# Mask rows, unread products and expert 0's input in place in attention; one pair of banks for transposed rows and rows in front of a block

## The chip, the core and the metric

The kernel runs on one core of one Trainium2 chip. Its engines work side by side, each through its own instructions in order: PE (TensorE, products and transposes; PEld are its weight loads), DVE (VectorE), ACT (ScalarE), POOL (GpSimd), and SP (SyncE), which here only issues DMA transfers. An engine that waits for something holds back all that stands behind in its program. The metric is the time of one execution in microseconds of the device, as a median of several runs. PE's clock has two levels, 1.2 and 2.4 GHz; the profile gives the granted one as a share of the higher.

## The reference, cut to what matters

Three layers in a row: attention in which a query sees only the keys of its own cluster, a mixture of 8 experts with one expert for each token, and a gated unit with a product before and after it.

```
q_assign = argmax(q_n @ c_n), k_assign = argmax(k_n @ c_n)      # 16 clusters, for each head
mask     = q_assign[:, :, :, None] == k_assign[:, :, None, :]
scores   = where(mask, q @ k.T / sqrt(64), -1e9)                # 2 x 8 heads, 768 x 768
x        = softmax(scores) @ v                                  # -> (1536, 512)
e        = argmax(x @ w_gate);  h = relu(x @ w1[e]);  y = gate * (h @ w2[e])    # 8 experts, 512 -> 1024 -> 512
out      = (silu(y @ wg) * (y @ wv)) @ wo                       # 512 -> 1536 -> 512
```

## The kernel before, in words

All arithmetic is in float32, made of float32r products of a high and a low part (names ending in H/L or h/l): a product is done as high times high plus the two mixed ones.

Attention takes the 16 heads as 8 pairs (n) of two heads (r). A head has six blocks of 128 queries; `run` (class Attention) goes through 96 of these blocks, called groups g: six of one head, then six of the other. In each group it emits steps in the order CFG['order']: S (`soft`: exponential of block g+1 on ACT), E (`evac`: result of three blocks, on ACT and DVE), Q (`qk`: score product of block g+2 on PE and its maximum on DVE), T0 and T1 (`pt`: transposes of the exponentials on PE, copied by ACT and DVE), B0 (first step of a list `bg[g]`), O (`onat`), V0 (`pv`, every third group: product with v), B1 (the other steps of `bg[g]`). A score product adds the mask by further rows of its operands: one-hot cluster rows in tiles Bq and Bk (qB, kB). For the second head of a pair these rows must stand on other partitions than the transposes leave them, so they are copied to a tile oT and moved by DMA (`move`, L150).

The list `bg` holds the preparation of pair n+1 (`prep_steps`: k0, q0, q1, k1 transposes of the loaded tiles ldq and ldk, L169; a, t, f the cluster choice; m0, m1 the mask rows), at offsets from CFG['offs'], for pair 1 from CFG['offs1'] (its q is prepared before the first group), and the load of the pair after it. k0 of pair 2 stands in group 9. Pair 0 is prepared ahead of the loop: `mask0` makes its mask rows, `unit` fetches the gate's weights by six small transfers, `moves` places the high and low parts of pair 1's q. `warm` emits products that nobody reads.

SP issues all moves and loads in program order. All of them are on one queue.

In groups 81 to 92 the weights of expert 0 arrive in eight chunks (raw tiles, a ring of NRAW = 4) and are split into high and low halves by `piece(i, k, eng)`: chunk i, half k, the high part copied by ACT (eng 1) or POOL (eng 0), the low part always made by POOL. The list `pieces` hangs at step E, `spare` at given groups. `head` fetches the first 128 tokens of expert 0 (which the router has scattered to moe_rows) into a raw tile, `turn_head` transposes them, `take_head` splits them into the tile XA. `tail` then computes these tokens (`head1`, `head2`) while the last tokens are scattered.

Experts (`run` of class Experts): for each expert four products l1, two l2, and between them `xt`, which transposes the rows of the next expert into two PSUM tiles of two banks each (a ring of four) and splits them into X. `split(e, i)` splits chunk i of expert e and then issues the load of the chunk four places on into the freed raw tile; `rows(e, t)` fetches rows of the expert after next. The gated unit (class Glu) follows.

Of the kernel before, what the change touches and what calls it, by code (L numbers as in the profile page):

```python
# [23 lines left out]
class Attention:  # L24
# [253 lines left out]
    def mask0(self):  # L278
# [23 lines left out]
        keys(*ps[1])  # L302
        queries(*ps[0])
        for sl, flat in ps:
            nc.vector.tensor_copy(st["oT"][q, sl], flat[q])
            nc.scalar.activation(out=st["oT"][k, sl], in_=flat[k], func=AF.Identity, scale=self.sc[k, 0:1],
                                 bias=self.sc[k, 1:2])
        for si, nm in enumerate("qk"):
            r0 = 2 * si * C
            self.move(st["B" + nm][64 - C:64, 1], st["oT"][r0 + C:r0 + 2 * C])  # L310

    def mask(self, n, half):
# [190 lines left out]
    def run(self, cent, gate, early, fill, after, spare, pieces, go):  # L503
# [6 lines left out]
        for n in range(1, self.NP):  # L510
            s0 = 2 * J * (n - 1)
            st = self.prep_steps(n)
            for nm, o in CFG["offs" if n > 1 else "offs1"]:
                if n == 1 and nm in ("q0", "q1"):
                    continue
                bg.setdefault(s0 + o, []).append(st[nm])
            if n + 1 < self.NP:
                bg.setdefault(s0 + CFG["load"], []).append(lambda n=n: self.load(n + 1, "qk"))
            if n > 1:
                bg.setdefault(s0 + 5, []).append(lambda n=n: self.load(n, "v"))  # L520
# [16 lines left out]
        self.warm(self.ps_m, "mm", 18)  # L537
        self.mask0()
        self.unit(gate)
        early()  # L540
        self.unit2()
        low()
        self.moves(1, 0, "q")
        self.moves(1, 1, "q")
        for e in range(self.E + 1):
# [4 lines left out]
        self.soft(0)  # L550
        self.qk(1)

        chains, moves, ready = [], [], {}
# [87 lines left out]

CFG = {'px': 'a', 'mt2': ['S', 'E', 'Q', 'T0'], 'mt': ['B1'], 'pt': 'V0', 'pe': 1, 'ms': [5, 2, 2], 'mr': 5, 'order': ['S', 'E', 'Q', 'T0', 'T1', 'B0', 'O', 'V0', 'B1'], 'offs': [['k0', -3], ['q0', -2], ['q1', -1], ['k1', 0], ['a', 1], ['t', 3], ['f', 6], ['m0', 7], ['m1', 8]], 'xe': 'da', 'me': 'a', 'ee': 'a', 'ec': 1, 'oc': [5, 5, 2], 'offs1': [['q0', 4], ['k0', 0], ['k1', 1], ['a', 2], ['t', 3], ['f', 5], ['m0', 6], ['m1', 7], ['q1', 0]], 'load': 0}

# [252 lines left out]
class Experts:  # L896
# [63 lines left out]

    def split(self, e, i):
        if e >= self.E:
# [5 lines left out]
        j = (nc.vector if e and i < 4 else nc.gpsimd).tensor_tensor(out=l, in0=t, in1=h.bitcast(F32), op=ALU.subtract)  # L968
        if e:
            for n in {8: [10], 9: [11], 10: [12], 11: [13], 12: [14, 15, 16]}.get(8 * e + i, [8 * e + i + NRAW]):  # L970
# [5 lines left out]
    def piece(self, i, k, eng):  # L976
# [7 lines left out]
        if k == 1:  # L984
            del self.loads[0, i]
            (lambda: self.load(4), self.head, self.slots, lambda: self.load(5), lambda: self.load(6), lambda: None,
             lambda: None)[i]()

    def head(self):

        rt = self.rt
        t = self.raw.tile([128, 4, 256], F32, tag="raw", name="raw").rearrange("p a b -> p (a b)")[:, 0:self.DM]
        i = self.nc.sync.dma_start(out=t, in_=rt.rows[rt.first:])
# [3 lines left out]
        self.xa = t  # L997

    def slots(self):
        self.XA = self.raw.tile([128, 2, self.KD, 128], F32R, tag="raw", name="XA")  # L1000

# [69 lines left out]
    def tail(self, at, go):  # L1071
# [17 lines left out]
        go(12)  # L1089
        a = self.fold(1)  # L1090
        rt.after(self.split(0, 7), [end])
        for _ in a:
# [66 lines left out]
    def xt(self, e, cnt):  # L1159
        nc = self.nc  # L1160
        banks = [self.bank("xp") for _ in range(self.KD // 2)]
        nt = 2 if self.late(e) else 3

        def turn(t, k):
            x = self.x3 if t == 2 else self.xr[e][:, t]
            return nc.tensor.transpose(banks[k // 2][:, k % 2, t * 128:(t + 1) * 128], x[:, k * 128:(k + 1) * 128], self.ident)

        def body(w):
            w = min(w, nt * 128)
            for a, b in ((0, 2), (2, 4)):  # L1170
                h, l = [self.X[:, i, a:b, 0:w] for i in range(2)]
                ps = banks[a // 2][:, a % 2:a % 2 + b - a, 0:w]
                nc.scalar.copy(out=h, in_=ps)
# [116 lines left out]
    def run(self, hook):  # L1290
# [5 lines left out]
        for e in range(E):  # L1296
# [5 lines left out]
            for mp in range(4):  # L1302
# [7 lines left out]
                if mp and mp < 3 and not e:  # L1310
                    self.split(1, mp - 1)
            if e:
                self.split(e, 6)
            if e == 5:
                rt.tokens(self.bank("xp")[:, 0, 0:2 * rt.B * rt.J])
            self.arms(e, cnt, lambda w: self.hidden(3, ps, w))
            if e + 1 < E:
                self.xt(e + 1, then)
                self.rows(e + 2, 0)
            if e:  # L1320
                self.split(e, 7)
# [181 lines left out]
def tile_clustered_attention_moe_swiglu(ctx, tc, q, k, v, cent, gate, w1, w2, wg, wv, wo, out, cap):  # L1503
# [7 lines left out]
    with tc.manual_schedule():  # L1511
        ident = const.tile([128, 128], F32, name="ident")
        with ExitStack() as c2:
# [3 lines left out]
            with ExitStack() as c1:  # L1517
# [12 lines left out]
                def first():  # L1530
# [8 lines left out]
                L = lambda i: lambda: ex.load(i)  # L1539
                pieces = [P(1, 1, 1), P(2, 0, 1), P(3, 1, 1), P(4, 0, 1), P(5, 1, 1), P(6, 0, 1)]  # L1540
                spare = {g0: [first], g0 + 1: [L(1), P(0, 0, 0)], g0 + 2: [L(2), P(0, 1, 0)], g0 + 3: [L(3), P(1, 0, 0)],
                         g0 + 5: [P(2, 1, 0)], g0 + 6: [P(3, 0, 0)], g0 + 8: [P(4, 1, 0)],
                          g0 + 9: [at.most, P(5, 0, 0), L(7)], g0 + 10: [lambda: None, lambda: ex.turn_head(at)],
                         g0 + 11: [ex.take_head, P(6, 1, 0)]}
                go = lambda n, it=ex.head1(at): [next(it) for _ in range(n)]
# [44 lines left out]
```

## Time and profile before

| | us |
|---|---|
| median of 3 runs | 753.95 (753.9 to 755.81) |
| profiled execution | 752.9 |
| its span | 751.2 |
| PE busy | 731.3 (97%) |
| DVE, ACT, POOL busy | 509.4, 394.5, 280.3 |
| granted clock of the span | 0.997 |

Attention takes the first 283 us of the span, the experts run until 446, the gated unit to the end. The span is the time between the first and the last instruction of the profile; the execution's own time is 1.7 us more. "Busy" counts an engine's instructions alone, so an engine can be 97% busy and slow all the same where its clock is halved. A row of the timeline gives the start, the duration, the engine, the line, the result and the operands, how many instructions were merged, and in brackets how long the engine stood idle before it and what ended that.

### The profile page before, as it was taken

Reading aid. Unit: us, or ns where it says so; the run is one execution under the profiler, and the core shown is the slowest. Engines: PE = TensorE matmul, PEld = TensorE weight load, DVE = VectorE, ACT = ScalarE, POOL = GpSimd, SP = SyncE. Lnnn points to the kernel's source line nnn. Section 1 sums busy time; section 2 is a strip of 40 time slices with the busy share of each in tenths; the row PEclk is TensorE's granted clock in tenths of the full one; section 3 lists DMA queues with packets and bytes.
Section 4 is the critical chain, followed back from the end, with each engine's and each line's share of the span. In section 5 each row is a group of like instructions: output and inputs, shape, how many; then the busy total and the mean of one; then the engine's idle time right before and its main releaser. Section 6 shows DMA issues by size and latency. Waiting matters only on the chain.

```text
span 751.2 us, 12723 instructions
## 1 busy us (share of the span) xinstructions
PE 731.3 (97%) x4310; PEld 608.7 (81%) x4310; DVE 509.4 (68%) x863; ACT 394.5 (53%) x763; POOL 280.3 (37%) x267
## 2 busy tenths in 40 slices
PE   7999999999999999999999999999999999999996
PEld 6777777767776789999999998788888888888885
DVE  4667777688787756666676567866766677676333
ACT  6777686877768754666667534542332222232110
POOL 6120211212125854555694334343333322333245
PEclk9999999999999999999999999999999999999999
DMA  9857869547256337688877733232122111210012
GB/s 203 176 137 205 203 181 250 129 108 173 48 157 205 101 125 241 220 253 267 264 248 239 217 116 106 89 89 80 57 67 74 57 57 56 85 29 0 1 57 112
DMA packets 103790, 102.92 MB, mean 137 GB/s; under 512 B 30896, under 2 KB 90800, under 8 KB 103696
## 3 DMA queue, kind: packets, MB, share of 16 engines
q1 hardware_dynamic: 101632, 95.37, 45.9%
q0 software_dynamic: 1920, 6.29, 2.2%
q8 instruction: 56, 0.92, 0.5%
q14 instruction: 38, 0.31, 0.1%
q10 hardware_dynamic: 144, 0.03, 0.0%
HBM read 68.48 MB, written 12.85 MB: 108 GB/s over the span
## 4 chain that ended last, share of the span: by engine, by line
PE 50%; DVE 4%; issue 3%; ACT 3%; POOL 1%; DMA 1%; DVEq 0%; ACTq 0%; POOLq 0%; SPq 0%
PE o L1456 12%; PE g L1438 12%; PE v L1438 12%; PE yp L1223 4%; PE hp L1223 3%; PE yp L1215 2%; PE hp L1215 2%; PE yp L1224 2%; PE hp L1224 1%; ACT W1h L967 1%; DVE gtmp L1415 1%; POOL out L1467 1%; DMA raw<-in_moe_w 1%; DVE gtmp L1414 0%; DVE hp L1237 0%
## 5 line engine op out<-in xcount | busy, mean ns | idle before, releaser
L368 DVE TENSOR_REDUCE nm<-s 128x1 f32<-128x768 f32 x96 | 91.1, 950 | 12.3 <-PE s L365 10.9
L968 POOL TENSOR_TENSOR W2l<-raw,W2h 128x1024 fp32r<-128x1024 f32 x29 | 69.1, 2396 | 66.8 <-ACT W2h L967 66.6
L378 ACT ACTIVATE P<-s,nm 128x768 f32<-128x768 f32 x96 | 86.6, 902 | 12.1 <-DVE nm L368 11.7
L397 PE MATMUL t<-ident,P 128*128 128x128 f32 x576 | 81.2, 275 | 0.9 <-ACT PT L400 0.7
L1445 POOL TENSOR_TENSOR ghl<-u,ghh 128x512 fp32r<-128x512 f32 x36 | 50.1, 1392 | 76.1 <-ACT ghh L1444 76.1
L397 PEld LDWEIGHTS t<-ident,P 128*128 128x128 f32 x576 | 68.9, 141 | 7.6 <-DVE PT L402 2.0
L416 PE MATMUL acc<-PT,ldv 128*64 128x384 f32 x384 | 69.2, 495 | 0.0
L1464 DVE TENSOR_TENSOR acc<-o,acc 128x512 f32<-128x512 f32 x60 | 41.5, 692 | 33.1 <-PE o L1456 32.9
L1223 PE MATMUL yp<-H,W2h 128*128 128x256 f32 (+3 forms) x224 | 61.7, 354 | 2.0 <-DVE H L1244 1.3
L365 PE MATMUL s<-Ak,Aq 128*128 128x384 f32 x192 | 58.8, 387 | 4.6 <-ACT P L378 3.8
L1223 PE MATMUL hp<-X,W1h 128*128 128x256 f32 (+3 forms) x224 | 61.0, 352 | 1.2 <-PE yp L1224 0.8
L1442 DVE TENSOR_TENSOR u<-sg,g 128x512 f32<-128x512 f32 x36 | 24.8, 688 | 54.8 <-ACT sg L1441 52.0
L400 ACT COPY PT<-t 128x384 f32<-128x384 f32 x96 | 45.7, 476 | 27.3 <-PE t L397 27.1
L1444 ACT CAST ghh<-u 128x512 fp32r<-128x512 f32 x36 | 22.4, 621 | 68.3 <-DVE u L1443 68.3
L1224 PE MATMUL yp<-H,W2l 128*128 128x128 f32 (+3 forms) x224 | 54.2, 242 | 0.0
L1224 PE MATMUL hp<-X,W1l 128*128 128x128 f32 (+3 forms) x224 | 54.0, 241 | 0.1
L402 DVE COPY PT<-t 128x384 f32<-128x384 f32 x96 | 52.4, 546 | 0.9 <-PE t L397 0.9
L968 DVE TENSOR_TENSOR W1l<-raw,W1h 128x1024 fp32r<-128x1024 f32 x28 | 43.3, 1565 | 13.8 <-ACT W1h L967 13.5
L365 PEld LDWEIGHTS s<-Ak,Aq 128*128 128x128 f32 x192 | 29.2, 190 | 28.6 <-ACT P L378 17.7
L365 PE MATMUL s<-kB,qB 80*128 80x384 f32 (+1 forms) x192 | 50.4, 343 | 0.3 <-issue 0.2
L416 PEld LDWEIGHTS acc<-PT,ldv 128*64 128x64 f32 x384 | 25.1, 136 | 28.0 <-issue 27.1
L176 POOL TENSOR_TENSOR Lk<-Xk,Hk 128x384 fp32r<-128x384 f32 x14 | 14.0, 1003 | 89.6 <-ACT Xk L175 89.6
(303 smaller groups left out, 1932.2 us busy)
## 6 DMA issues: line engine op xcount, KB each, us to landing
raw<-in_moe_w SPq DMA_DIRECT2D x64, 512.0 KB, 5.0
Ak<-Hk SPq DMA_DIRECT2D x32, 192.0 KB, 4.4
moe_rows<-zero SPq DMA_DIRECT2D x8, 768.0 KB, 5.3
raw<-in_moe_w_gate SPq DMA_DIRECT2D x12, 512.0 KB, 3.6
raw<-in_moe_w_val SPq DMA_DIRECT2D x12, 512.0 KB, 3.8
raw<-in_moe_w_out SPq DMA_DIRECT2D x12, 512.0 KB, 3.6
xr<-moe_rows SPq DMA_DIRECT2D x17, 256.0 KB, 4.1
ldq<-in_q SPq DMA_DIRECT2D x16, 192.0 KB, 4.1
```

The lines of the kernel that those rows point to most:

```text
L365: nc.tensor.matmul(ps[:, c, 0:HS], lhsT=ql[:, qs], rhs=kr[:, c * HS:(c + 1) * HS], start=a == 0, stop=a == 1)
L368: nc.vector.tensor_reduce(out=nm, in_=ps[:, :, 0:HS], axis=AX.XY, op=ALU.max, negate=True)
L378: nc.scalar.activation(out=P, in_=ps[:, :, 0:HS], func=AF.Exp, bias=nm, accum_out=self.pairs[n]["sum"][:, i, r:r + 1])
L397: nc.tensor.transpose(ps[:, jj, :], P[:, a, jj * 128:(jj + 1) * 128], self.ident)
L402: nc.vector.tensor_copy(PT[:, js, cs], ps)
L416: nc.tensor.matmul(acc[c * D:(c + 1) * D], lhsT=v[:, c * HJ + j], rhs=PT[:, c * HJ + j, :], start=j == 0, stop=j == HJ - 1, tile_position= ...
L968: j = (nc.vector if e and i < 4 else nc.gpsimd).tensor_tensor(out=l, in0=t, in1=h.bitcast(F32), op=ALU.subtract)
L1223: self.nc.tensor.matmul(out[:, :, 0:w], lhsT=W[0][:, k, cols], rhs=mov[:, :, k, 0:w], start=k == 0, stop=False)
L1224: self.nc.tensor.matmul(out[:, 0, 0:w], lhsT=W[1][:, k, cols], rhs=mov[:, 0, k, 0:w], start=False, stop=k == ks - 1)
L1438: nc.tensor.matmul(ps[which], lhsT=W[a], rhs=self.Y[b][:, k, ts], start=k + i == 0, stop=k == KD - 1 and i == 2)
L1445: nc.gpsimd.tensor_tensor(out=hl[:, fc], in0=u, in1=hh[:, fc].bitcast(F32), op=ALU.subtract)
L1456: nc.tensor.matmul(p[t], lhsT=h[a][:, fc, t * 128:(t + 1) * 128], rhs=W[b][:, fc], start=fc == 0 and i == 0, stop=fc == 1 and i == 2)
```

## The change

Five edits:

- `mask0` yields: the transposes and the rows of the first head are emitted ahead of the loop as before, the copies to oT in two halves as steps of groups 0 and 1, its two moves in group 1. `unit` and the moves of pair 1's q go behind them, in group 1. The other steps for pair 1 stand one group later, and the load of pair 2 two groups later.
- Nine unread products follow the second score product.
- The load of expert 0's first tokens goes into the second half of the tile XA, which is later overwritten by the low part. `pieces` loses chunk 6's first half, which POOL now copies in group 92; its second half goes to `tail`, copied by ACT.
- `split(e, 6)` keeps its load back until the rows of the next expert are transposed and the rows of the one after are asked for.
- `xt` of experts with two row tiles uses one PSUM tile: four slots of 256 columns in two banks.

```diff
@@ mask0
         queries(*ps[0])
+        yield
         for sl, flat in ps:
             nc.vector.tensor_copy(st["oT"][q, sl], flat[q])
...
+            if sl.start == 0:
+                yield
         for si, nm in enumerate("qk"):
             r0 = 2 * si * C
             self.move(st["B" + nm][64 - C:64, 1], st["oT"][r0 + C:r0 + 2 * C])
+        yield
@@ Attention.run
-                bg.setdefault(s0 + CFG["load"], []).append(lambda n=n: self.load(n + 1, "qk"))
+                bg.setdefault(s0 + CFG["load"] + 2 * (n == 1), []).append(lambda n=n: self.load(n + 1, "qk"))
...
-        self.mask0()
-        self.unit(gate)
+        masks = self.mask0()
+        next(masks)
         early()
         self.unit2()
         low()
-        self.moves(1, 0, "q")
-        self.moves(1, 1, "q")
+
+        def rest():
+            next(masks)
+            self.unit(gate)
+            self.moves(1, 0, "q")
+            self.moves(1, 1, "q")
+
+        bg.setdefault(0, []).insert(0, lambda: next(masks))
+        bg.setdefault(1, []).insert(0, rest)
...
         self.qk(1)
+        self.warm(self.ps_t, "t", 9)
@@ CFG
-'offs1': [['q0', 4], ['k0', 0], ['k1', 1], ['a', 2], ['t', 3], ['f', 5], ['m0', 6], ['m1', 7], ['q1', 0]]
+'offs1': [['q0', 4], ['k0', 1], ['k1', 2], ['a', 3], ['t', 4], ['f', 6], ['m0', 7], ['m1', 8], ['q1', 0]]
@@ Experts.split
-    def split(self, e, i):
+    def split(self, e, i, held=None):
...
-        if e:
+        if held is not None:
+            held.append(8 * e + i + NRAW)
+        elif e:
@@ Experts.piece, head
-            (lambda: self.load(4), self.head, self.slots, lambda: self.load(5), lambda: self.load(6), lambda: None,
+            (lambda: self.load(4), self.head, lambda: None, lambda: self.load(5), lambda: self.load(6), lambda: None,
...
-        t = self.raw.tile([128, 4, 256], F32, tag="raw", name="raw").rearrange("p a b -> p (a b)")[:, 0:self.DM]
+        self.XA = self.raw.tile([128, 2, self.KD, 128], F32R, tag="raw", name="XA")
+        t = self.XA[:, 1].rearrange("p k t -> p (k t)").bitcast(F32)
...
-    def slots(self):
-        self.XA = self.raw.tile([128, 2, self.KD, 128], F32R, tag="raw", name="XA")
@@ Experts.tail
         a = self.fold(1)
+        self.piece(6, 1, 1)
         rt.after(self.split(0, 7), [end])
@@ Experts.xt
-        banks = [self.bank("xp") for _ in range(self.KD // 2)]
         nt = 2 if self.late(e) else 3
+        if nt == 2:
+            at = self.bank("xp").rearrange("p b (m t) -> p (b m) t", m=2)
+        else:
+            banks = [self.bank("xp") for _ in range(self.KD // 2)]
...
-            return nc.tensor.transpose(banks[k // 2][:, k % 2, t * 128:(t + 1) * 128], x[:, k * 128:(k + 1) * 128], self.ident)
+            to = at[:, k] if nt == 2 else banks[k // 2][:, k % 2]
+            return nc.tensor.transpose(to[:, t * 128:(t + 1) * 128], x[:, k * 128:(k + 1) * 128], self.ident)
@@ Experts.run
+            held = []
             if e:
-                self.split(e, 6)
+                self.split(e, 6, held)
...
             if e + 1 < E:
                 self.xt(e + 1, then)
                 self.rows(e + 2, 0)
+            for n in held:
+                self.load(n)
@@ tile_clustered_attention_moe_swiglu
-                pieces = [P(1, 1, 1), P(2, 0, 1), P(3, 1, 1), P(4, 0, 1), P(5, 1, 1), P(6, 0, 1)]
+                pieces = [P(1, 1, 1), P(2, 0, 1), P(3, 1, 1), P(4, 0, 1), P(5, 1, 1)]
...
-                         g0 + 11: [ex.take_head, P(6, 1, 0)]}
+                         g0 + 11: [ex.take_head, P(6, 0, 0)]}
```

## Rows read from the trace of the kernel before

**Rows 1.** The page's first part: busy us, share of span, instructions.

```profile
PE 731.3 (97%) x4310; PEld 608.7 (81%) x4310; DVE 509.4 (68%) x863; ACT 394.5 (53%) x763; POOL 280.3 (37%) x267
```

**Rows 2.** Windows: stretch, length, busy by engine, PE's granted clock, DMA share, GB/s.

```profile
19.00:20.00 1.00, 1.00 (x7) 0.95 (x6) 0.69 (x1) 0.12 (x2) 0.00 (x0) 0.51 0.89 194
...
22.00:23.00 1.00, 1.00 (x8) 0.90 (x7) 0.43 (x1) 1.00 (x4) 0.83 (x1) 0.78 0.85 283
...
290.00:294.00 4.00, 2.98 (x23) 2.56 (x23) 3.06 (x7) 2.11 (x5) 2.32 (x4) 1.00 0.54 152
```

**Rows 3.** Timeline of PE at the start.

```profile
10.82 2.13 PE L501 MATMUL warm<-ident 128*128 128x128 f32 x18
...
18.24 0.62 PE L365 MATMUL s<-Ak,Aq 128*128 128x384 f32 x2 [1.40 <-ACT P L378]
...
23.25 0.59 PE L365 MATMUL s<-Ak,Aq 128*128 128x384 f32 x2
...
42.10 0.49 PE L169 MATMUL trp<-ident,ldk 128*128 128x128 f32 x3
...
46.33 0.60 PE L365 MATMUL s<-Ak,Aq 128*128 128x384 f32 x2
...
48.03 0.62 PE L365 MATMUL s<-Ak,Aq 128*128 128x384 f32 x2
```

**Rows 4.** Timeline of DVE and ACT at the start.

```profile
15.28 1.01 DVE L305 CAST oT<-otp 32x384 fp32r<-32x384 f32 x2
...
15.87 1.22 ACT L306 ACTIVATE oT<-otp,sc 32x384 fp32r<-32x384 f32 x2 [0.38 <-DVE oT L305]
...
19.30 0.96 DVE L368 TENSOR_REDUCE nm<-s 128x1 f32<-128x768 f32 x1 [1.28 <-PE s L365]
...
20.59 0.56 DVE L402 COPY PT<-t 128x384 f32<-128x384 f32 x1 [0.32 <-PE t L397]
...
24.29 0.91 ACT L378 ACTIVATE P<-s,nm 128x768 f32<-128x768 f32 x1
```

**Rows 5.** SP's issues; then issue to landing of ldk (33 to 42) and oT.

```profile
21.12 0.57 SPq L150 DMA_DIRECT2D qB<-oT  x1
...
26.40 0.60 SPq L150 DMA_DIRECT2D Aq<-Hq  x1
...
39.08 0.60 SPq L150 DMA_DIRECT2D kB<-Lk  x1
...
DMA to landing us min/median/max: 3.8/4.1/4.4
...
DMA to landing us min/median/max: 2.9/3.1/3.2
```

**Rows 6.** Windows of the start: DMA share and GB/s are the last columns.

```profile
28.00:29.00 1.00, 1.00 (x10) 0.43 (x6) 0.96 (x3) 0.64 (x2) 0.00 (x0) 1.00 0.94 206
...
42.00:43.00 1.00, 1.00 (x10) 0.65 (x10) 1.00 (x2) 0.82 (x2) 0.00 (x0) 1.00 0.48 100
```

**Rows 7.** Timeline of group 91 and 92, end of attention.

```profile
254.53 0.55 DVE L402 COPY PT<-t 128x384 f32<-128x384 f32 x1
...
254.69 0.62 ACT L982 CAST W2h<-raw 128x512 fp32r<-128x512 f32 x1 [1.65 <-DMA raw<-in_moe_w]
...
255.33 0.48 ACT L400 COPY PT<-t 128x384 f32<-128x384 f32 x1
...
255.86 0.88 PE L397 MATMUL t<-ident,P 128*128 128x128 f32 x6 [0.71 <-ACT PT L400]
```

**Rows 8.** Timeline of the tail, where expert 0's first tokens are computed.

```profile
275.97 0.59 ACT L1053 COPY hA<-ha 128x512 f32<-128x512 f32 x1 [1.54 <-PE ha L1023]
...
275.93 2.40 POOL L968 TENSOR_TENSOR W2l<-raw,W2h 128x1024 fp32r<-128x1024 f32 x1
...
277.40 0.22 PE L1023 MATMUL ya<-HA,W2l 128*128 128x128 f32 x1
```

**Rows 9.** Experts: PE after a branch, SP's rows, and a window.

```profile
318.19 0.40 PE L1223 MATMUL hp<-X,W1h 128*128 128x352 f32 x1 [0.77 <-PE yp L1224]
...
332.78 0.45 SPq L1151 DMA_DIRECT2D xr<-moe_rows  x1
...
350.00:360.00 10.00, 10.00 (x73) 10.00 (x72) 7.37 (x8) 5.65 (x9) 3.34 (x2) 1.00 0.77 251
```

More of the change, by code (lines that the diff above doesn't have):

```diff
@@ L639, in run @@
             pass
-CFG = {'px': 'a', 'mt2': ['S', 'E', 'Q', 'T0'], 'mt': ['B1'], 'pt': 'V0', 'pe': 1, 'ms': [5, 2, 2], 'mr': 5, 'order': ['S', 'E', 'Q', 'T0', 'T1', 'B0', 'O', 'V0', 'B1'], 'offs': [['k0', -3], ['q0', -2], ['q1', -1], ['k1', 0], ['a', 1], ['t', 3], ['f', 6], ['m0', 7], ['m1', 8]], 'xe': 'da', 'me': 'a', 'ee': 'a', 'ec': 1, 'oc': [5, 5, 2], 'offs1': [['q0', 4], ['k0', 0], ['k1', 1], ['a', 2], ['t', 3], ['f', 5], ['m0', 6], ['m1', 7], ['q1', 0]], 'load': 0}
+CFG = {'px': 'a', 'mt2': ['S', 'E', 'Q', 'T0'], 'mt': ['B1'], 'pt': 'V0', 'pe': 1, 'ms': [5, 2, 2], 'mr': 5, 'order': ['S', 'E', 'Q', 'T0', 'T1', 'B0', 'O', 'V0', 'B1'], 'offs': [['k0', -3], ['q0', -2], ['q1', -1], ['k1', 0], ['a', 1], ['t', 3], ['f', 6], ['m0', 7], ['m1', 8]], 'xe': 'da', 'me': 'a', 'ee': 'a', 'ec': 1, 'oc': [5, 5, 2], 'offs1': [['q0', 4], ['k0', 1], ['k1', 2], ['a', 3], ['t', 4], ['f', 6], ['m0', 7], ['m1', 8], ['q1', 0]], 'load': 0}
 class Router:
@@ L1171, in body @@
                 h, l = [self.X[:, i, a:b, 0:w] for i in range(2)]
-                ps = banks[a // 2][:, a % 2:a % 2 + b - a, 0:w]
+                ps = at[:, a:b, 0:w] if nt == 2 else banks[a // 2][:, a % 2:a % 2 + b - a, 0:w]
                 nc.scalar.copy(out=h, in_=ps)
```

## The prediction

> **What bounds the kernel now.** I read the page's first part: the product engine PE is busy for 97% of the span [rows 1]. So a change pays only where PE is idle or slow, and costs where it makes PE wait. Then the windows of the start, which show the one stretch where PE's clock was halved [rows 2]. Then the timeline by engine around each place that the diff touches: PE and the two engines that read its results at the start [rows 3, 4], the SP queue with its transfers [rows 5, 6], the tail of attention where expert 0's weights are split [rows 7, 8], and the experts [rows 9]. The gated unit after them is untouched and PE stands without a gap there, so every shift before it arrives at the end unchanged.
>
> Times below are those of the profiled execution: 752.9 us in all, of which 751.2 are span. The median of the runs is 753.95, 1.05 above; I add the sum to the median.
>
> **Part 1: the nine unread products.** After the second score group PE has nothing until the first softmax block is read: the next score product starts at 18.24 after 1.40 us of idle time [rows 3]. From 19 the granted clock is then 0.51 and in the two microseconds after that 0.50, and in the fourth 0.78: 1.2 instead of 2.4 GHz for 3.4 us [rows 2]. Eighteen such transposes took 2.13 us [rows 3], so nine take 1.07: they end near 17.9, before 18.24, and delay nothing. The idle time falls to some 0.3 us, and I take it that the clock stays up. What the half clock cost: two groups of scores, transposes and one turn of inputs took 5.01 us (18.24 to 23.25), against 1.70 for one at full clock (46.33 to 48.03) [rows 3]. That is 1.6 us, the most that this part can bring; the least is nothing.
>
> **Part 2: the mask rows of the second head.** The four copies that make them (two of DVE, 1.01 us; two of ACT, 1.22 us) stood before the first block, where DVE ends at 16.29 and ACT at 17.09 [rows 4]. There they cost some 0.1 us, as the first score products and their maximum end at about these times. Now half of them stand behind the transposes of group 0, half behind those of group 1. ACT has less room there. Adding 0.6 us to each of the two groups, I place its exponential of block 3 near 23.2 (24.29 before [rows 4]), so that PE gains not 1.6 but about 0.9 us by group 4, of which 0.4 is a set of transposes that the change moves one group later. Left: 0.5 us, bounds 0 and 1.6.
>
> **Part 3: what stands behind these rows on SP.** Here lies the price. The two moves of the mask rows were issued from 21.12 on, right behind the values of pair 1 [rows 5]. SP works in order, and now it must wait for the second half of the copies. On DVE: maximum of group 2 until 20.26 (row), transposed half 0.56, first mask half 0.50, maximum of group 3 0.96, transposed half 0.56, second mask half 0.50 [rows 4]: 23.3. So SP stands idle for 2.2 us, and everything behind it starts 2.2 later: the two moves, six tiny gate transfers, then sixteen transfers of 192 KB. Those sixteen start at 26.40, and the last is issued at 39.08 [rows 5]; the DMA share is 0.94 from 28 on and halves at 42 [rows 6], so they are bound by the transfers themselves, and no order of them makes the last one earlier. Now they start at 28.6, and the last is issued near 41.3.
>
> And their order changes. Before: six moves of q of pair 1, four loads of pair 2, six moves of k. The load step goes from group 0 to group 2, behind the turn of k. After: six, six, four. The last of the sixteen was a move that pair 1's first score group needs, in group 10; the last is now a load of pair 2's k. Its first user is earlier: the transposes at 42.10, in group 9 [rows 3]. The load had 4 us to spare there: it was issued before the six moves of k, near 33.6, and such loads landed 3.8 to 4.4 after their issue [rows 5]. Now: by bytes, the end of the DMA stretch (42.2 less the four small transfers, say 41.8) plus 2.2 gives 44.0; by issue and landing, 41.3 + 3.8 gives 45.1; the early end is 43.4. I take 44.0, since the queue drains behind it. PE would arrive near 41.5 (42.10 less the 0.5 of part 2). It waits 2.5 us with group 9's products and all later ones behind it, and stands at 44.0 instead of 42.1: +1.9 (bounds +1.3 and +3.0). The gain of parts 1 and 2 vanishes in this wait. The mask rows of pair 1 come behind the loads (near 43.2, landing 2.9 to 3.2 later by [rows 5]), before their user at 46.4.
>
> A wait of 2.5 us is longer than the 1.40 that preceded the half clock; a stretch with 1.02 us of idle time kept the clock [rows 2]. The nearest row is that of 1.40, so I take another stretch of half clock, at the price of part 1: +1.6 (bounds 0 and 1.7, half of the 3.4 us). Together +3.5 for the start.
>
> The Trainium skill (DMA: Bandwidth & Descriptors, section Where 436 GB/s comes from) gives the fabric a ceiling of 435 GB/s. By it, an estimate, the sixteen would need 7.2 us and land with 5 us to spare, and part 3 would cost nothing; the trace moved 206 GB/s at a DMA share of 0.94 [rows 6], so I go by the trace.
>
> **Part 4: expert 0's input in place, and its weight piece.** In group 91 ACT had to split the first half of weight chunk 6 and waited 1.65 us for its transfer; the transposed copy behind it came at 255.33, and PE stood 0.71 us [rows 7]. This half now goes to POOL one group later, so ACT's copy comes at about 253.7, and the 0.71 are gone. Next in line is DVE's copy of the other half, whose end at 255.08 lets PE go on some 0.05 later: -0.7 (bounds -0.3 and -0.8). The input tile written over its own load changes no instruction, and its copies lie under 2 us of products. The second half goes to the tail: ACT 0.6 us, under its 1.54 us of idle time [rows 8]; POOL half of the 2.40 us that a whole chunk took, and some overhead, from 275.93: ready near 277.2, while its first user comes at 277.40 [rows 8]. That is tight, 0 to 0.2. POOL's split of the last chunk then ends at 279.6 instead of 278.3, two us before its user. The slots of the ring of four serve the same loads as before, since the input tile and its load now share one. Nothing else moves.
>
> **Part 5: one pair of banks, rows ahead of a block.** The transposed rows keep their eight transposes, two copies and two subtractions of the same size; PE had finished with the pair that is freed, and no product waits for a bank. The block that was loaded ahead of the rows waited on SP for POOL's split; now the rows go first, 3 to 4 us earlier than 332.78, but their user comes in the next expert, and PE is busy 10.00 of 10 us from 350 to 360 [rows 9]. Both cost nothing; as the code is laid out anew, waits of PE at a branch for nothing that the profile shows (0.77 us at 318.19) [rows 9] may move: bounds -0.3 and +0.3.
>
> **Sum.** +1.9 + 1.6 - 0.7 = +2.8: 755.7 as profiled, 756.7 as median.
>
> **Rivals.**
> - *The clock holds through the wait.* For it: 1.02 us of idle time in four did not bring it down [rows 2]. Against it: 1.40 did. +1.9 - 0.7 = +1.2: 755.2.
> - *The load lands in time* (the other side: not slower). The mechanism is that the loads, no longer mixed with moves and drawn from memory alone, pass faster than the 206 GB/s of the stretch, so that SP can issue the sixteen at the 0.60 us of the first one [rows 5]: the last at 37.6, landing 3.8 later at 41.4. It decides from a landing before 41.5. For it: the first transfers of the stretch were issued at that pace. Against it: the DMA share is near 1 by 28 and stays there [rows 6]. Then -0.5 - 0.7 = -1.2: 752.8. The ceiling of the Trainium skill's page on DMA, named above, would bring this about.
> - *The load lands in time and ACT follows*, so that the whole half-clock loss returns: -1.6 - 0.7 = -2.3: 751.6. Against it: the mask copies that ACT now has to fit in before its row at 24.29 [rows 4].
> - *The unread products don't do what they should*: the clock falls at 19 all the same, as PE also idles before 15. Then the mask copies and all of SP come some 0.9 us later: 2.8 + 0.9 = +3.7: 757.6.
>
> **Chances.** Forecast 0.42, clock holds 0.16, load in time 0.25, with ACT following 0.09, no effect of the products 0.08. About 0.3%, 2.3 us, is what a measurement of this kernel tells from no change: below 751.7 or above 756.2. Faster: two thirds of the fourth case and a tail of the third, with the bounds of part 4: 0.14. Slower: three quarters of the forecast, the last case and a tail of the second: 0.40. Same: 0.46. The range from 752.0 to 758.0 leaves out most of the fourth case and tails at both ends, 0.2. As cases of both signs hold much of the chance: the forecast's own range is 755.6 to 758.0.
>
> **What would show it.** Right: granted clock 1.00 from 19 to 23; SP's move of the mask rows near 23.3; the last load of k issued past 40.5; PE idle for about 2.5 us before the transposes of group 9, with DMA as its releaser, and half clock after it; no idle time before the transposes at 255. Wrong: transposes of group 9 near 41.5 without a wait (part 3 falls, and the result is below 753.5); half clock at 19 (part 1 falls); PE idle at 277 (part 4 was mis-sized); a different time of the experts from 300 to 446 (part 5 falls).

## The result, and the profile after

The changed kernel is slower: 761.59 us (median of six runs, 758.57 to 763.0) against 754.17 for the kernel before on the same chips, a ratio of 1.0081 with a 95% interval of 1.006 to 1.0102. The prediction had 756.7 and a range up to 758.0. The profiled execution took 759.37 us with a span of 757.7, so +6.5 against 752.9 before. The forecast sum was +2.8: the sign was right, the size was not.

The page's first part looks as before [rows 1]: PE is busy for 97%. The loss is not in this line.

```profile
PE 733.7 (97%) x4319; PEld 610.7 (81%) x4319; DVE 508.8 (67%) x863; ACT 394.3 (52%) x763; POOL 280.1 (37%) x267
```

The timeline of PE after, from the start to the tail of attention (start, duration, engine, line, operation, and in brackets the idle time before it with its releaser):

```profile
15.86 0.84 PE L369 MATMUL s<-kB,qB 80*128 80x384 f32 x2 [0.37 <-DMA kB<-Lk]
...
17.78 1.95 PE L505 MATMUL warm<-ident 128*128 128x128 f32 x9
19.49 0.60 PE L369 MATMUL s<-Ak,Aq 128*128 128x384 f32 x2
...
23.10 0.55 PE L169 MATMUL trp<-ident,ldk 128*128 128x128 f32 x3 [0.60 <-ACT oT L307]
24.12 0.61 PE L369 MATMUL s<-Ak,Aq 128*128 128x384 f32 x2 [0.47 <-ACT P L382]
...
27.09 0.62 PE L369 MATMUL s<-Ak,Aq 128*128 128x384 f32 x2 [1.02 <-ACT P L382]
...
46.66 0.87 PE L169 MATMUL trp<-ident,ldk 128*128 128x128 f32 x3 [2.42 <-DMA ldk<-in_k]
47.46 3.47 PE L420 MATMUL acc<-PT,ldv 128*64 128x384 f32 x12
...
50.86 0.62 PE L369 MATMUL s<-Ak,Aq 128*128 128x384 f32 x2
...
261.30 0.82 PE L401 MATMUL t<-ident,P 128*128 128x128 f32 x6
...
284.35 0.39 PE L1034 MATMUL ya<-HA,W2h 128*128 128x256 f32 x1 [0.64 <-DVE HA L1068]
```

Of the kernel before, beside [rows 3]:

```profile
42.52 2.16 PE L416 MATMUL acc<-PT,ldv 128*64 128x384 f32 x12
44.61 0.62 PE L365 MATMUL s<-Ak,Aq 128*128 128x384 f32 x2
```

Read the first list against these. The third score product comes at 19.49 in place of 18.24. The transposes of pair 2's k, in group 9, come at 46.66 in place of 42.10: +4.56, behind a wait of 2.42 us for the load. The twelve products behind them ran at half clock (3.47 us in place of 2.16), and the score product for block 12, at 44.61 before, stands at 50.86: +6.25. This difference is called the offset of the two traces below. From here to 187 us it stays between +6.2 and +6.3. At the transposes that had waited 0.71 us [rows 7] it is +5.44 (261.30), with no wait. It is +5.2 at 318, +6.2 at 354, +7.7 at the gated unit's first product (453.89 for 446.17), and +6.5 from its second stage to the end. So: start +6.25, attention's end and tail -1.1, experts +1.3.

The windows after (PE's granted clock, DMA share and GB/s are the last three columns), against [rows 2]:

```profile
16.00:17.00 1.00, 1.00 (x4) 1.00 (x5) 0.26 (x1) 0.00 (x0) 0.75 (x3) 0.51 0.97 297
18.00:19.00 1.00, 1.00 (x6) 1.00 (x6) 0.96 (x1) 0.72 (x2) 0.00 (x0) 0.50 0.95 206
19.00:20.00 1.00, 1.00 (x8) 1.00 (x7) 0.00 (x0) 0.99 (x2) 0.00 (x0) 0.79 1.06 231
46.00:48.00 2.00, 1.34 (x5) 0.77 (x7) 0.00 (x0) 0.43 (x2) 0.00 (x0) 0.68 0.28 52
48.00:50.00 2.00, 2.00 (x8) 0.72 (x6) 0.00 (x0) 1.32 (x4) 1.00 (x1) 0.50 0.00 0
50.00:52.00 2.00, 2.00 (x14) 1.29 (x10) 0.46 (x1) 0.48 (x1) 0.00 (x0) 0.96 0.00 0
```

The clock fell at 16, three microseconds earlier than before and ahead of the nine products, which ran at half clock for that reason (1.95 us). It was back from 20 on, and fell once more behind the load's wait.

DVE, ACT and SP at the start, after, against [rows 4, 5]:

```profile
21.81 0.54 DVE L306 CAST oT<-otp 32x384 fp32r<-32x384 f32 x1
...
23.61 0.54 DVE L306 CAST oT<-otp 32x384 fp32r<-32x384 f32 x1
```

```profile
22.39 0.66 ACT L307 ACTIVATE oT<-otp,sc 32x384 fp32r<-32x384 f32 x1 [1.10 <-DVE oT L306]
23.07 0.90 ACT L382 ACTIVATE P<-s,nm 128x768 f32<-128x768 f32 x1
...
24.46 0.67 ACT L307 ACTIVATE oT<-otp,sc 32x384 fp32r<-32x384 f32 x1
```

```profile
24.17 0.57 SPq L150 DMA_DIRECT2D qB<-oT  x1
...
29.76 0.59 SPq L150 DMA_DIRECT2D Aq<-Hq  x1
...
42.08 1.31 SPq L138 DMA_DIRECT2D ldk<-in_k  x1
```

ACT's mask copy waits 1.10 us for DVE's copy of the same half, and the softmax block of group 2 stands behind it on ACT. SP reaches the mask rows' move at 24.17, right behind DVE's second mask copy (23.61 + 0.54), the sixteen transfers at 29.76, and the last load of k at 42.08. This load landed 4.5 us later, near 46.6, where PE's wait ends.

### The profile page after: what moved, and what is told of

It reads as the page before. It is cut to its first block, busy times and chain, and to the rows that moved or that the text cites. A ratio compares the mean times of both kernels' runs of the same rounds, so it can differ in the third digit from the quotient of the medians.

```text
span 757.7 us, 12742 instructions
## 1 busy us (share of the span) xinstructions
PE 733.7 (97%) x4319; PEld 610.7 (81%) x4319; DVE 508.8 (67%) x863; ACT 394.3 (52%) x763; POOL 280.1 (37%) x267
## 4 chain that ended last, share of the span: by engine, by line
PE 47%; DVE 4%; issue 4%; ACT 3%; POOL 2%; DMA 1%; POOLq 0%; ACTq 0%; DVEq 0%
PE o L1476 12%; PE g L1458 12%; PE v L1458 12%; PE hp L1240 3%; PE yp L1240 2%; PE hp L1232 2%; PE yp L1232 2%; DMA raw<-in_moe_w 1%; PE hp L1241 1%; PE yp L1241 1%; ACT W1h L979 1%; DVE gtmp L1435 1%; POOL out L1487 1%; POOL W2l L980 1%; ACT W2h L979 0%
## 5 line engine op out<-in xcount | busy, mean ns | idle before, releaser
L1484 DVE TENSOR_TENSOR acc<-o,acc 128x512 f32<-128x512 f32 x60 | 41.5, 692 | 33.1 <-PE o L1476 32.9
L369 PEld LDWEIGHTS s<-Ak,Aq 128*128 128x128 f32 x192 | 29.3, 190 | 28.1 <-ACT P L382 17.5
L980 DVE TENSOR_TENSOR W1l<-raw,W1h 128x1024 fp32r<-128x1024 f32 x28 | 41.4, 1494 | 14.5 <-ACT W1h L979 14.2
```

Source lines behind the costliest of these rows:

```text
L369: nc.tensor.matmul(ps[:, c, 0:HS], lhsT=ql[:, qs], rhs=kr[:, c * HS:(c + 1) * HS], start=a == 0, stop=a == 1)
```

## The experiments

Ratios are against the kernel before on the same chip, with 95% intervals; 0.0013 is one microsecond. The kernel before alone ran between 751.0 and 759.3 us in these sessions.

**The change in two halves.** `start_only` has the diff down to CFG, `rest_only` all behind it.

```
start_only: mask0, run, CFG as changed   | split, piece, head, xt, pieces as before
rest_only:  mask0, run, CFG as before    | split, piece, head, xt, pieces as changed
```

> The kernel before with the edits of the start alone: mask rows in the loop, nine unread products, pair 1 one group later, load of pair 2 two groups later; expert 0 and the experts as before. Theory T1 (the start costs all): the score product of group 12's queries stands 6.2 us later than before, as in the changed kernel, and nothing gives it back, so +6 to +6.5 us against before (ratio 1.008). Theory T2 (the experts' edits cost as much as the start): +4 or less. In both the profile should show the wait of some 2.4 us for the load of k of pair 2 in group 9.

> The kernel before with the other edits alone: expert 0's input in place, its weight piece, one pair of banks, rows in front of the load; the start as before. T1 (these edits are small): -0.9 us in attention's last groups, and 0 to +1.5 behind them, so -0.9 to +0.6 us. T2 (they cost): the offsets of the two traces grow by 1.1 us over the experts (from +5.2 at 318 to +6.3 at 388), and by one more near 446, so +0.5 to +1.5. Prediction on record: -0.7.

Measured: `start_only` 759.15, ratio 1.0067 (1.0041 to 1.0092); `rest_only` 754.85, 1.0004 (0.998 to 1.0028). The start holds nearly all of it, as T1 has it; the interval of `rest_only` is too wide to choose between its own two theories. In the trace of `start_only` the wait in group 9 is 2.37 us and the offset +6.2 from behind it to 187, as in the changed kernel:

```profile
46.70 0.90 PE L169 MATMUL trp<-ident,ldk 128*128 128x128 f32 x3 [2.37 <-DMA ldk<-in_k]
```

**The load back at group 0.**

```diff
-    bg.setdefault(s0 + CFG["load"] + 2 * (n == 1), []).append(lambda n=n: self.load(n + 1, "qk"))
+    bg.setdefault(s0 + CFG["load"], []).append(lambda n=n: self.load(n + 1, "qk"))
```

> The changed kernel with the load of pair 2 back at group 0, so that its four transfers are issued near 21.7, while SP would else stand and wait for the mask rows' copies; all else as changed. T1 (the late load makes the wait in group 9 and the second stretch of half clock): no wait before the transposes of pair 2's k, granted clock 1.00 from 44 to 52, 3.5 to 4.3 us less than the changed kernel (ratio against before near 1.003). T2 (the lag of DVE and ACT behind the mask copies is the cause and the load only shows it): within 1 us of the changed kernel.

Measured: 756.0, 1.0016 (0.9994 to 1.0039), against 1.0081: 4.9 us of the loss. The timeline of PE with the early load:

```profile
16.88 1.15 PE L505 MATMUL warm<-ident 128*128 128x128 f32 x9
18.42 0.62 PE L369 MATMUL s<-Ak,Aq 128*128 128x384 f32 x2 [0.39 <-ACT P L382]
...
43.03 0.49 PE L169 MATMUL trp<-ident,ldk 128*128 128x128 f32 x3
43.45 2.16 PE L420 MATMUL acc<-PT,ldv 128*64 128x384 f32 x12
```

In group 9 there is no wait, and the clock is full (2.16 us for the twelve products in place of 3.47). The four loads were issued from 21.11 to 23.9, in the time in which SP stood and waited. T1 holds.

**The late load alone.** The edit is the change's own form of that line (with `+ 2 * (n == 1)`), put into the kernel before.

> The kernel before with the load of pair 2 two groups later and nothing else. SP still reaches the mask rows' moves at 21.12 and the last of the sixteen transfers at 39.1. T1 (the load's loss comes from order and SP's wait together, and each alone is small): the load of k lands near 42.5 to 43.2, PE waits 0.3 to 1.0 us before the transposes of group 9, +0.3 to +1.0 us. T2 (the order alone is the loss): PE waits 2 us or more there, +3 or more. Prediction on record counted order and wait together.

Measured: 756.16, 1.0007 (0.9989 to 1.0025). T2, with +3 or more, is out. The wait that T1 expected didn't show in the profiled execution, since PE was itself 4.75 us late there (for the reason, see the last section), so its size isn't shown. By the ratios the late order alone costs some 0.5 us, the change with the early load 1.2 (`load_first`), the change with both the late order and SP's wait 6.1.

**Without the nine products; with them alone.**

```diff
         self.qk(1)
-        self.warm(self.ps_t, "t", 9)
```

> The changed kernel without the nine unread products. T1 (they come too late, since the clock has fallen before them, and they run 1.7 us at half clock in front of the third score product): the third score product comes about 1.2 us earlier, near 18.3, but the clock stays down longer; the time is 0 to 1.5 us less than the changed kernel. T2 (they bring the clock back early, as meant): 1 to 2 us more than the changed kernel, with half clock until about 22.5.

> The kernel before with the nine unread products alone. T1 (the prediction's part 1): they run at full clock from some 16.8 to 17.9, end before 18.24 and the granted clock stays 1.00 from 18 to 24, so -1.6 us. T2 (they come behind the wait that decides, which lies ahead of the first score products near 15, 0.7 to 1.3 us for the landing of Aq): the clock falls before or with them in some executions, they then take 1.95 us in place of 1.07, and the time stays within 0.7 us of before.

Measured: without them the changed kernel takes 760.1, 1.008 (1.0056 to 1.0104), the same as with them; the intervals leave room for both theories. In the trace T1's earlier score product is there (18.44), the clock falls with it (0.70 from 18 to 19, 1.00 again from 22), and PE reaches group 9 at nearly the same time:

```profile
46.83 0.55 PE L169 MATMUL trp<-ident,ldk 128*128 128x128 f32 x3 [2.52 <-DMA ldk<-in_k]
47.30 2.16 PE L420 MATMUL acc<-PT,ldv 128*64 128x384 f32 x12
```

In both the load's landing sets the time in group 9, whatever came before it. In the kernel before, the products alone gain: 752.67, 0.9972 (0.9957 to 0.9988), 2.1 us, on T1's side. The trace of that run can't show it stage by stage, since its first products ran slow.

The starts of the other profiles show more. Of those whose first products ran at full speed, six have no unread products behind the second score product, and in all six the granted clock fell to half between 17.8 and 19.0. It stayed there for 3.4 us in the kernel before and in `no_products`, and for 6.8 us in `rest_only`, `masks_only`, `xt_only` and `xt_order`. Five have the products: in the changed kernel and `start_only` the clock fell at 16, ahead of them; in `load_first`, `one_engine` and `best_b` it did not fall, and the nine took 1.15 us. So in these profiles they keep the clock up where it has not fallen before them. The profile of the kernel before is a mild case: from 18.24 to 23.25 of its time, PE lost 1.1 to 1.4 us more in `rest_only`, `xt_only` and `xt_order`, which have the same start.

**The mask copies.** `masks_only` is the kernel before with the moved mask rows, the gate's weights and pair 1's steps, with the early load and without the products. `one_engine` is the changed kernel with the early load and one instruction in place of two:

```diff
-            nc.vector.tensor_copy(st["oT"][q, sl], flat[q])
-            nc.scalar.activation(out=st["oT"][k, sl], in_=flat[k], func=AF.Identity, scale=self.sc[k, 0:1],
-                                 bias=self.sc[k, 1:2])
+            nc.vector.tensor_scalar(out=st["oT"][0:4 * C, sl], in0=flat[0:4 * C], scalar1=self.sc[0:4 * C, 0:1],
+                                    scalar2=self.sc[0:4 * C, 1:2], op0=ALU.mult, op1=ALU.add)
```

> The kernel before with the mask rows' copies, the gate's weights and pair 1's steps moved as in the change, but the load of pair 2 at group 0 as before, no unread products and nothing of the other edits. T1 (the copies in the loop are a cost of their own, since ACT's waits 1.1 us for DVE's and the next softmax block stands behind it): PE waits some 2 us for P and oT between 18 and 28, +1.5 to +3 us against before. T2 (the copies cost nothing, all of the start's loss is the load): within 0.7 of before. Prediction on record: a gain of 0.5 for parts 1 and 2 together.

> The changed kernel with the load of pair 2 at group 0, and DVE making both halves' mask rows with one instruction each, so that ACT copies none. T1 (ACT's wait for DVE and its copies set the pace of groups 0 to 4): no wait of ACT before oT, the block of group 2 some 1.3 us earlier, PE's waits for P and oT from 18 to 28 fall by 1.5 us or more, and so does the time against the changed kernel with the load alone moved (ratio near 1.000). T2 (the pace is set by DVE or the transposes): within 0.7 of that kernel (1.0016).

Measured: `masks_only` 757.22, 1.0026 (1.0006 to 1.0045): +2.0 (0.5 to 3.4), T1. In its trace PE waits 2.7 us for P between 18 and 28, 1.4 in the kernel before. Against `rest_only`, `xt_only` and `xt_order`, whose clock was at half for as long, its PE stands 0.8 to 1.1 us later at 30, less than the median has. `one_engine` 754.18, 0.9992 (0.9973 to 1.0011), 1.8 below the kernel with the load alone moved, though the intervals overlap. What PE waited for between 18 and 42, first with the load alone moved, then with DVE's single copies (us in total, times, longest):

```profile
PE s L369 <- ACT P L382: 2.2, 4, 1.0
PE trp L169 <- ACT oT L307: 0.6, 1, 0.6
PE t L401 <- DVE PT L406: 0.5, 1, 0.5
```

```profile
PE s L368 <- ACT P L381: 0.8, 3, 0.4
PE t L400 <- DVE PT L405: 0.5, 1, 0.5
```

2.0 us of waits are gone, as T1 expected, and ACT begins the softmax block of group 2 at 20.30 in place of 22.03.

**Expert 0 alone, and its tail mended.** `expert0_only` has the diff of `piece`, `head`, `tail` and `pieces`. `best_d` is `best_b` (below) with one engine changed:

```diff
-        nc.gpsimd.tensor_tensor(out=l[:, ks], in0=t[:, ks], in1=h[:, ks].bitcast(F32), op=ALU.subtract)
+        (nc.vector if (i, k) == (6, 1) else nc.gpsimd).tensor_tensor(out=l[:, ks], in0=t[:, ks], ...)
```

> The kernel before with expert 0's edits alone (input in place, chunk 6's first half to POOL one group later, its second half in the tail). T1 (as in the changed kernel's trace): the 0.71 us before the transposes at 255.86 go, 0.9 us gained until 264, of which a wait of PE for DVE's HA of 0.6 us near 279 takes back two thirds: -0.3 to -0.9. T2 (the tail and the loads that follow lose more): 0 or above.

> The version with the three mends, and the low part of chunk 6's second half made by DVE in place of POOL. T1 (in the tail a subtraction of two SBUF operands on POOL holds DVE's counting step of two SBUF operands, 1.90 us for 16 columns in place of 0.18, and DVE's copies of the products behind it come late): all four counting steps take 0.18, and PE's wait of 0.7 us for HA is gone or below 0.3, so -0.4 to -0.7 us. T2 (the wait comes from ACT's copies in the tail): the wait stays at 0.6 or more.

Measured: `expert0_only` 754.69, 1.0003 (0.9982 to 1.0024): nothing that can be measured, and no choice between the two theories. Its trace gains 0.9 us at the transposes (offset +3.2 to +2.3) and has the wait of 0.64 for HA. That wait starts here, in the tail of the changed kernel, DVE first and then POOL:

```profile
279.39 0.60 DVE L838 TENSOR_TENSOR roff<-roff 128x16 f32<-128x16 f32 x3
...
280.02 1.90 DVE L838 TENSOR_TENSOR roff<-roff 128x16 f32<-128x16 f32 x1
...
282.25 0.69 DVE L1066 TENSOR_TENSOR ha<-ha,hA 128x512 f32<-128x512 f32 x1
```

```profile
280.58 1.29 POOL L997 TENSOR_TENSOR W2l<-raw,W2h 128x512 fp32r<-128x512 f32 x1
```

The counting steps (`roff`) add up the experts' token counts. Three took 0.18 us each, the fourth 1.90: it ended at 281.92, 0.05 behind POOL's subtraction. (Its record begins 0.56 before that of the subtraction; spans on POOL are rough.) In `best_b` the instruction behind it was caught (2.00 us in place of 0.17). All ten profiles with this subtraction on POOL have one such DVE instruction of 1.90 to 2.00 us, which ends 0.03 to 0.05 behind the subtraction, and a wait of PE for HA of 0.63 to 0.71; the other seven have neither. With the low part on DVE:

```profile
275.88 0.81 DVE L837 TENSOR_TENSOR roff<-roff 128x16 f32<-128x16 f32 x4
...
277.01 0.69 DVE L996 TENSOR_TENSOR W2l<-raw,W2h 128x512 fp32r<-128x512 f32 x1
278.07 0.70 DVE L1065 TENSOR_TENSOR ha<-ha,hA 128x512 f32<-128x512 f32 x1 [0.37 <-ACT hA L1064]
```

PE has no wait for HA left, and gains 0.7 there on `best_b` (whose trace it trails by 3.95 ahead of this place and 3.23 behind it). T1 holds for the mechanism. The whole time, 753.26 with 0.9971 (0.9951 to 0.999), can't tell 0.7 us.

**The single pair of banks.** `xt_only` is that edit in the kernel before. `xt_order` is `rest_only` with both copies first where the single pair is used (`nt == 2`):

```diff
+            todo = []
             for a, b in ((0, 2), (2, 4)):
...
+                if nt == 2:
+                    todo.append((l, ps, h))
+                    nc.scalar.copy(out=h, in_=ps)
+                    continue
                 nc.scalar.copy(out=h, in_=ps)
+                nc.vector.tensor_tensor(out=l, in0=ps, in1=h.bitcast(F32), op=ALU.subtract)
+            for l, ps, h in todo:
                 nc.vector.tensor_tensor(out=l, in0=ps, in1=h.bitcast(F32), op=ALU.subtract)
```

> The kernel before with one pair of banks for the transposed rows alone. T1 (the shared tile makes ACT's second copy wait for DVE's first subtraction, 0.5 to 0.7 us in each of six experts, so that ACT and DVE run later and PE waits for DVE's H and at the end for Yl): +1.0 to +1.5 us, with PE's wait for Yl of 1.1 us at the gated unit. T2 (the held load is what costs): within 0.3 of before. Prediction on record: 0.

> All edits of expert 0 and of the experts, none of the start, but in xt with one pair of banks both copies of ACT are emitted ahead of both subtractions of DVE. T1 (the order copy, subtraction, copy, subtraction on one tile is the cost): ACT's copies stand back to back, no idle time of ACT before X, 1.0 to 1.5 us less than the same edits with the order as changed, so -0.9 to 0 against before. T2 (the held load or the smaller ring costs): no better than those edits, +0.5 to +1.5.

Measured: `xt_only` 756.16, 1.0021 (1.0003 to 1.0039), +1.6 (0.2 to 2.9), T1. `xt_order` 753.34, 0.9983 (0.9964 to 1.0002), 1.6 below `rest_only` by the ratios, though the intervals overlap. ACT's copies between 300 and 440 (line, shapes, count; busy us, mean ns; idle time before and its releaser), first `xt_only`, then `xt_order`:

```profile
L1177 ACT CAST X<-xp 128x416 fp32r<-128x416 f32 (+1 forms) x12 | 6.6, 558 | 3.4 <-DVE X L1178 3.4
```

```profile
L1181 ACT CAST X<-xp 128x416 fp32r<-128x416 f32 x10 | 4.6, 516 | 0.1
L1183 ACT CAST X<-xp 128x768 fp32r<-128x768 f32 x2 | 1.5, 815 | 0.0
```

In the kernel before, on two tiles, ACT waited 0.2 us in all. On one tile the second copy waits for the first subtraction, though they read other columns; with both copies first the wait is gone. The offset to the kernel before over the experts (from 290 to 480 of its time) agrees: it grew by 0.7 to 4.7 us in the six profiles with one tile in the order as changed, by -1.2 to +1.2 in the four with the mended order, by -1.4 to +2.0 in the six with two tiles. Single waits of other kinds are part of this scatter, such as 1.76 us for rows at 408 in `one_engine`, with half clock behind it.

Where ACT's idle time reaches PE is less clear. PE's waits in the changed kernel, in the experts and at the gated unit:

```profile
PE yp L1240 <- DVE H L1261: 2.8, 5, 1.0
PE g L1458 <- DVE Yl L1272: 1.1, 1, 1.1
```

The first stood at 1.3 before and 1.0 in `xt_order`, but at 3.2 in `best_b`, which has the mended order too, so it does not follow the order alone. The second was not there before and stays with the mended order, so the order is not its cause; the gated unit gives it back by its second stage (+7.7 to +6.5).

**Versions put together.** `best_a`: start as before with the nine products, other edits with `xt_order`. `best_b`: the whole change with the early load, DVE's single mask copies and `xt_order`. `best_c`: `best_b` with xt as before.

```
best_a = xt_order + self.warm(self.ps_t, "t", 9)
best_b = changed kernel + load at group 0 + one_engine's copies + xt_order's copies
best_c = best_b, xt with two pairs of banks
```

> What the runs so far hold to be good: the start as before with the nine unread products, expert 0's edits, the held load, and one pair of banks with both copies ahead of both subtractions. If the two gains add (0.9972 for the products, 0.9983 for the rest): ratio 0.9955, some 3.3 us less than before. If they don't: 0.997.

> All edits of the change with the three mends: load of pair 2 at group 0, mask rows by DVE alone, both copies ahead of both subtractions in xt. T1 (the three are the whole loss): below before, 0.996 to 0.999. T2 (moving the mask rows into the loop costs by itself): 1.000 or above, and slower than the version whose start is as before.

> The version with the three mends, but with xt as before (two pairs of banks). T1 (the single pair of banks also shifts the ring of four, so that the gated unit's first product waits 1.13 us for DVE's Yl, most of which the unit takes back at its second stage): no wait for Yl, 0.2 to 0.6 us less than the mended version. T2 (the mended single pair is worth something by itself): 0.3 or more above it.

Measured: `best_a` 753.53, 0.9975 (0.9952 to 0.9998); `best_b` 752.11, 0.9969 (0.9948 to 0.999); `best_c` 755.28, 1.0003 (0.9981 to 1.0024). `best_b` beats both kernels, as its T1 has it: by the ratios some 2.3 us below the one before and 8.4 below the changed one. The nine products alone, at 0.9972, do as well within the intervals, so no gain of the other edits is shown. `best_a`'s gains did not add to the 0.9955 expected. In `best_c` the wait for Yl is gone, as T1 said, but its time lies 2.6 us above `best_b`, on T2's side, though the intervals overlap: no cost of the ring's rotation is shown.

## Why the prediction was wrong

**Part 3 was right in its mechanism and wrong in its size; it is the term that failed.** Forecast: the load of k lands at 44.0 and PE stands +1.9 there. Measured: near 46.6 and +4.56. Three things made the 2.6. Of the two landings that the text worked out, I took 44.0, by the bytes, and not 45.1, by issue and landing: 1.1. The last load was issued at 42.08 and not 41.3: 0.8. It landed 4.5 after its issue and not 3.8: 0.7; 3.8 was the least of the landing times read before, and this trace has 4.3 to 4.9 for the four loads. Issue and landing was the right way to count, and its bound of +3.0 the nearer one, but still too low. The late issue comes from the clock: the third score product stood at 19.49, behind products at half clock, so DVE's maximum and both mask copies behind it were late, and SP's move of the mask rows was at 24.17 and not at 23.3. In `load_first`, at full clock, the second mask copy ended at 23.1, as the text has it. That the wait itself was sized well, 2.42 against 2.5, is luck: PE came at 44.24, 2.7 later than the 41.5 of the text, and the load 2.6 later. The half clock behind it cost 1.7 (+4.56 to +6.25), against 1.6. The rival that the load lands in time is out; the sixteen took 16.9 us from first issue to last landing (29.76 to 46.6), and moving the load back gave 4.9 us.

The estimate by the Trainium skill (DMA: Bandwidth & Descriptors, section Where 436 GB/s comes from) would have had the sixteen need 7.2 us. The trace doesn't agree: they took 16.9 us, so the ceiling gives no time for this queue.

**Part 2 had the wrong sign.** Forecast: the mask copies in the loop leave a gain of 0.5 with the products. Measured: they cost 2.0 by themselves (0.5 to 3.4) by the median of the runs, 0.8 to 1.1 by traces with as much half clock. I added durations on each engine and missed that ACT's copy waits for DVE's copy of the same half, 1.10 us, with the softmax block behind it: ACT began the exponential of block 3 at 26.05, where the text has 23.2. The row of 0.38 us in [rows 4] showed that very wait. In the changed kernel the load's landing comes later than this delay of PE and covers it; what is left of it there is SP's lateness.

**Part 1 holds alone, not in the change.** The products bring 2.1 us to the kernel before and nothing to the changed one. In the changed kernel's profile the clock was not at 1.00 from 19: it had fallen at 16, ahead of the products. In `load_first`, where it had not fallen, they did what the text says: they ended at 18.03, the third score product came at 18.42, at full clock. The most that I gave, 1.6, is the price of the 3.4 us in one profile; four other profiles without the products have 6.8 us at half clock. The rival "the unread products don't do what they should", with 757.6, came nearest, and its 0.9 us for SP was right (0.87, 24.17 for 23.3). It fell short because it kept the landing of the forecast.

**Part 4 was right where it looked.** The wait of 0.71 us is gone and ACT's copy early. I checked POOL's half chunk against its own user, and not against DVE beside it: behind the held counting step PE waited 0.64.

**Part 5 failed.** It was costed at 0 with a bound of 0.3, since the operations have the same size. Their order on one tile was the cost, 1.6 us alone (0.2 to 2.9).

In sum, by the traces: start +6.25 for +3.5, expert 0 and tail -1.1 for -0.7, experts +1.3 for 0 (one pair of profiles, within the scatter named above). The runs' median lies 2.2 above the profiled execution, where the text added 1.05.

## What to carry to other kernels

When a step is moved, follow each DMA behind it to its landing by the last issue of its kind plus the time from issue to landing, and look for the user of whatever becomes last on the queue. Two engines that copy halves out of one tile in turn may be put in a row by the program: let one engine do it, or emit all copies of the first engine ahead of the second's. A small edit beside a queue's wait can be hidden by that wait, so take the wait away before judging the edit. One profile is one execution: before a stretch of half clock goes into a sum, see in others how often it comes and how long it lasts.

## What the runs showed of the hardware that was not expected

- A subtraction with two SBUF operands on POOL held a DVE instruction with two SBUF operands: 1.90 and 2.00 us in place of 0.18 and 0.17. It was so in all ten profiles with that subtraction. DVE's `ha` took its 0.70 us under POOL's 2.40 in the kernel before; one of its operands is in PSUM. The Trainium skill (GPSIMD Engine Reference, section 1. Specifications) says that POOL shares its SBUF interfaces with VectorE, with contention for DVE instructions of two SBUF inputs; these rows agree.
- The clock does not follow from the length of a wait. Behind 2.42 and 2.37 us it fell (the changed kernel, `start_only`), behind 2.52 it stayed at 1.00 (`no_products`). At 16 it fell in the changed kernel and in `start_only` behind waits of 0.96 and 0.37, 0.93 and 0.49, and not in `load_first` or `one_engine` behind 1.24 and 1.27. What decides stays open.
- In six of the seventeen profiles PE's products took nearly twice as long up to about 17.5, and PE stood 3.4 to 3.8 us late at the first score products. The row below is from `products_only`; in the kernel before the same twelve products took 1.42.

```profile
8.31 2.61 PE L263 MATMUL t<-cbd,Xq 128*128 128x32 f32 x12
```

The traces of these six hold no record of the granted clock before 17.3 to 17.7, those of the other eleven none before 4.2 to 6.0; a window without a record prints 1.00. So the 1.00 there says nothing, and the clock is likely at half up to the first record; that is an inference from the durations. It came in kernels with and without the change, and may be much of the scatter of the runs; that was not tested.
